# Where three V products stand behind stage A and D items, and an unfolded stage D for batch 2

## The chip, the cores and the metric

One Trainium2 chip, one core. The time is what the device takes for one execution of the whole program, in microseconds (us); less is better. Each kernel has several runs, and their median stands for it. One further execution was taken by the hardware profiler; all views of the trace are of that one.

## The reference

The input x is (8, 3072, 256) in float32. The first half takes the real part of a two-dimensional Fourier transform of each batch (over the 3072 positions and the 256 features); the second half is a channel mix on its result:

```
X   = fft(fft(x, axis=1), axis=2).real
xk  = mu_k * X + (1 - mu_k) * X_prev      # X_prev: X moved on by one position, zeros first
xr  = mu_r * X + (1 - mu_r) * X_prev
k   = relu(xk @ w_k)                      # 256 -> 1024
v   = (k * k) @ w_v                       # 1024 -> 256
out = sigmoid(xr @ w_r) * v
```

## The kernel before, in words

**The channel mix** is the bulk of the work and sets the beat. A batch has 3072 positions, in six chunks of 512 (`chunks`, line 997: 48 in all, three of the first half of the positions and three of the mirrored half per batch). A chunk takes four steps, so there are 192 steps and a few more to empty the pipeline. In every step TensorE makes one *K piece* (`k_piece`, lines 830 to 837): four products of 512 columns, two of the chunk's eight blocks of k, into one psW buffer. ScalarE (ACT) empties that with a relu into `rl`. Every second step VectorE (DVE) squares two steps' worth of `rl` into `k2` (`square`, line 845). Five steps behind, every step has a *V tile* (`v_tile`, lines 859 to 867): eight products of 256 columns for 128 positions, which read `k2` of an earlier chunk. Its first four products read the first half of `k2`, its last four the second half; so the first V tile of a chunk (steps 21, 25, 29, ...) waits for the latest square. Two V tiles share a psV buffer, and `v_out` (line 888) multiplies them with the sigmoid `r` on VectorE and issues the output DMAs. Every fourth step has an `r_item` (eight products, one sigmoid on ACT). PSUM is held as three psW buffers of 1024 columns, taken in turn by K pieces, r items and all transform items, and two psV buffers of 512.

**The transform** of later batches is cut into items and put between these steps. `fold` (line 160) adds a row of x to its mirrored partner (`p`). From `p`, `quarters_1` and `quarters_2` (lines 177 to 202, six VectorE operations per half h) fold the features twice more; `butterfly` (line 205, two operations per half) folds them once. Both write `eo`. Stage A (`a_half`, line 610, with `a_slots_0`) multiplies `eo` with half-array products (48 of 128 rows) and evicts to `a`, once per (h, e). Stage D turns `a` into `g_all`. It has two forms: `d_half` (line 672), for input folded twice, with products of 64 rows, two row halves of the array side by side, and two ACT evictions per item; it needs the table `w_d`, which `quarter_tables` (line 549) builds with one product, four ACT copies and two VectorE memsets on row 64. The other is `d_item` (line 665), for input folded once, with products of all 128 rows and one eviction per item. Batch 1 uses `d_item` and `butterfly`, batches 2 to 7 `d_half` and the quarters. `turned` (line 692) is one small product on `g_all` and an ACT copy. Stage C (`c_pairs`, line 738) makes `pq`; `halves` (line 751) adds and subtracts its two parts on VectorE to y, `diff` (line 762) takes differences of y, and `mix` (lines 770 to 813) makes from y and these the x that K pieces and r items read.

**The order** is written out by hand. `at(step, ...)` puts an item into a step, in class "x" if it uses TensorE (behind the K piece, ahead of the V tile) and else in class "w" (VectorE work and loads, at the step's end). `event(step, ...)` puts a stretch of stage A, C or D items behind the V tile of its step. The loop at lines 1140 to 1164 issues, per step: K piece, x items, V tile, event items, w items, output, square. After an event of three items the V tile of the *next* step follows at once: `event` then adds that step to `early_v` (line 995), and the loop skips it at its own place. An event that begins with `a_slots_0` is left out of that rule. `EVENTS` (line 1001) gives the steps of a batch's events, from 24 b for the transform of batch b + 2: 29 (three D items), 33 (the fourth, two C items), 41 (two C items and the first A item of the next batch), 45 (the other three A items). `pin_order` keeps each engine to the order of issue.

Of the kernel before, what the change touches and what calls it, by code (L numbers as in the profile page):

```python
# [39 lines left out]
def kernel(  # L40
# [916 lines left out]
    for a in range(2):  # L957
        t = x_t["t", a] = mix_pool.tile([P, 24, 64], FP16, name=f"t{a}")
# [25 lines left out]
    def at(step, f, *args):  # L984
        work.setdefault((step, "x" if f in (a_item, a_sum, d_item, d_small, c_item, c_tiles, turned, minus_0, r_item, quarter_tables) else "w"),
                        []).append((f, args))
# [3 lines left out]
    early_v = set(range(17, 20))  # L990

    def event(step, *items):
        work.setdefault((step, "e"), []).extend((f[0], f[1:]) for f in items)
        if len(items) > 2 and items[0][0] is not a_slots_0:
            early_v.add(step + 1)
# [5 lines left out]
    EVENTS = (29, 33, 41, 45)  # L1001
# [64 lines left out]
    at(17, c_tiles, 1)  # L1066
    at(17, fold, 2, 0)
    event(18, (c_item, 1, 0, 8), (c_item, 1, 8, 8))
    at(18, quarters_1, 2, 0)
    at(19, quarters_2, 2, 0)  # L1070
    at(18, fold, 2, 1)
    event(20, (c_item, 1, 16, 8), (c_item, 1, 24, 4), (a_half, 2, 0, 0))
    at(19, diff, 1, 0, 12)
    at(20, r_item, (0, 1, 1))
    at(23, a_half, 2, 0, 1)
    at(20, mix, 1, 0, 0, 0, 0, 12)
    at(21, quarters_1, 2, 1)
    at(22, quarters_2, 2, 1)
    at(21, mix, 1, 0, 0, 1, 0, 12)
    at(22, diff, 1, 12, 26)  # L1080
    at(21, load_gate)
# [6 lines left out]
    at(26, mix, 1, 0, 1, 0)  # L1088
    event(27, (a_slots_0, 2), (a_half, 2, 1, 0), (a_half, 2, 1, 1))
    at(28, r_item, (1, 0, 0))  # L1090
    at(28, mix, 1, 0, 1, 1)
    at(22, quarter_tables)
    at(30, mix, 1, 1, 1, 0)
    at(31, mix, 1, 1, 1, 1)
    at(32, r_item, (1, 0, 1))
    for n, c in enumerate(chunks[8:]):
        at(4 * n + 36, r_item, c)
    for b in range(B):
        s0 = 24 * b

        for n, st0 in enumerate((2, 4, 6, 8) if b > 1 else ()):
            at(s0 + st0, mix, b, n // 2, 1, n % 2)
        if b and b + 3 < B:
            at(s0 + 22, load_gate)
            for h in range(2):
                at(s0 + 22, load_xh, b + 3, h)
        t = b + 2
        if t < B:
            if b:
                at(s0 + 9, fold, t, 0)  # L1110
                at(s0 + 10, quarters_1, t, 0)
                at(s0 + 11, quarters_2, t, 0)
                at(s0 + 12, fold, t, 1)
                at(s0 + 14, quarters_1, t, 1)
                at(s0 + 15, quarters_2, t, 1)
            c = [(c_pairs, t, 8 * n, (8, 8, 8, 4)[n], "A") for n in range(4)]
            d = [(d_half, t, n) for n in range(4)]
            a = [(a_half, t + 1, h, e) for h in range(2) for e in range(2)] if t + 1 < B else []
            at(s0 + 32, turned, 0, 12)
            at(s0 + 37, turned, 12, 13)  # L1120
            event(s0 + EVENTS[0], *d[:3])
            event(s0 + EVENTS[1], d[3], *c[:2])
            event(s0 + EVENTS[2], *c[2:], *a[:1])
            if a:
                event(s0 + EVENTS[3], (a_slots_0, t + 1), a[2], a[3], a[1])
        t = b + 1
        if b and t < B:
            at(s0 + 16, halves, t, 0, 15)
            at(s0 + 18, halves, t, 15, 27)
            for a in range(2):  # L1130
                at(s0 + 19 + a, diff, t, 0, 26, (a,))
                at(s0 + 21 + a, mix, t, 0, 0, a)
            at(s0 + 24, mix, t, 1, 0, 0)
            at(s0 + 25, mix, t, 1, 0, 1)
# [62 lines left out]
```

## Time and profile before

| | |
|---|---|
| median of 3 runs | 434.36 us (433.93 to 434.51) |
| profiled execution | 434.02 us, span 432.2 us |
| granted TensorE clock, mean | 0.999 |
| PE busy | 421.7 us, 4018 matmuls |
| VectorE busy | 371.3 us, 594 instructions |
| ScalarE busy | 329.8 us, 414 instructions |
| DMA | 42.08 MB, mean 97 GB/s |

The span runs from the first to the last instruction; the 1.8 us beside it lie around the program. A view of the trace names an instruction by engine, line of the kernel, operation, and output and input tiles. PE is TensorE's products, ACT is ScalarE, DVE is VectorE. In a timeline the columns are start and length in us, then the engine, line and operation, the shapes, how many instructions were put together, and in brackets how long the engine sat idle before the first and what ended that. Products on PE are pipelined, so what one costs is read from start to start, not from its length. In the list of waits the numbers are us in total, times, and the longest. In a row of stretches the numbers are the stretch, its length, and the busy time of each engine with its instructions in brackets (PE, weight loads, VectorE, ScalarE, GpSimd), the clock, and the DMA share and rate; with a line of the kernel chosen, only that line's engine is given. In a row of a group, the numbers behind the bar are busy us and mean ns of one.

### The profile page before, as it was taken

What the parts mean: (1) busy time and instruction counts of PE and PEld (TensorE: products, weight loads), DVE (VectorE), ACT (ScalarE), POOL (GpSimd) and SP (SyncE); (2) the same over time, 40 slices, a digit from 0 to 9 for tenths busy, and PEclk for the clock granted to TensorE, in tenths of its full rate; (3) what the DMA queues carried; (4) which work ended last, traced back from release to release, by engine and by line L of the source; (5) the groups of instructions that cost most, each with busy time, mean ns of one, the idle gap of its engine ahead of it and who ended that gap; (6) DMA issues with size and microseconds to landing.
All of it is one profiled execution on the core that took longest, in us unless ns stands there. A gap on an engine that the chain in (4) does not pass through costs nothing.

```text
span 432.2 us, 9708 instructions
## 1 busy us (share of the span) xinstructions
PE 421.7 (98%) x4018; PEld 294.5 (68%) x4018; DVE 371.3 (86%) x594; ACT 329.8 (76%) x414; POOL 62.3 (14%) x97
## 2 busy tenths in 40 slices
PE   8999999999999999999999999999999999999996
PEld 3767766667666776766677677667766766766775
DVE  8999999999987999979989899888998756997543
ACT  7889897886878878687786967778686887666661
POOL 7488402000050002300041000500000000000000
PEclk9999999999999999999999999999999999999999
DMA  8789956323385224932368223762332323223333
GB/s 174 103 121 197 219 124 129 75 53 70 74 155 137 52 63 80 193 78 57 76 116 175 66 55 69 146 146 52 73 74 49 74 52 73 61 65 73 70 75 97
DMA packets 35104, 42.08 MB, mean 97 GB/s; under 512 B 4114, under 2 KB 31092, under 8 KB 35060
## 3 DMA queue, kind: packets, MB, share of 16 engines
q1 hardware_dynamic: 27488, 25.41, 24.2%
q0 software_dynamic: 7264, 15.80, 21.8%
q8 instruction: 31, 0.51, 0.5%
q10 hardware_dynamic: 308, 0.26, 0.2%
q14 instruction: 13, 0.11, 0.1%
HBM read 32.08 MB, written 25.17 MB: 132 GB/s over the span
## 4 chain that ended last, share of the span: by engine, by line
PE 88%; DVE 5%; ACT 4%; issue 1%; POOL 0%; POOLq 0%; DVEq 0%
PE psW L825 36%; PE psV L866 33%; PE psW L852 9%; PE psV L878 3%; ACT g_all L574 2%; PE psW L746 1%; DVE k L845 1%; ACT a L574 1%; PE psW L235 1%; PE psW L679 1%; DVE x L790 1%; DVE o L888 1%; PE psW L635 1%; DVE t L779 1%; PE psW L617 1%
## 5 line engine op out<-in xcount | busy, mean ns | idle before, releaser
L835 ACT ACTIVATE rl<-psW 128x1024 f16<-128x1024 f32 x192 | 194.3, 1030 | 85.7 <-PE psW L825 80.8
L825 PE MATMUL psW<-x,wk 128*128 128x512 f16 (+1 forms) x776 | 194.9, 377 | 3.4 <-ACT a L574 2.8
L866 PE MATMUL psV<-wv_sb,k 128*128 128x256 f16 x1424 | 184.7, 273 | 1.5 <-DVE k L845 1.5
L866 PEld LDWEIGHTS <-k 128*128 128x128 f16 x1424 | 136.6, 98 | 41.9 <-DVE k L845 2.3
L845 DVE TENSOR_TENSOR k<-rl 128x2048 f16<-128x2048 f16 (+1 forms) x100 | 115.6, 1157 | 37.1 <-ACT rl L835 36.8
L825 PEld LDWEIGHTS <-wk 128*128 128x128 f16 x776 | 75.3, 98 | 58.4 <-issue 5.1
L888 DVE SCALAR_TENSOR_TENSOR o<-psV,r 128x512 f32<-128x512 f32 (+1 forms) x97 | 65.8, 681 | 11.7 <-PE psV L866 10.6
L790 DVE TENSOR_TENSOR x<-y,t 128x1536 f16<-128x1536 f16 (+3 forms) x74 | 62.1, 846 | 2.1
L852 PE MATMUL psW<-wr,x 128*128 128x256 f16 x384 | 49.8, 273 | 0.0
L857 ACT ACTIVATE r<-psW 128x1024 f16<-128x1024 f32 x48 | 48.9, 1019 | 0.8 <-PE psW L852 0.8
L852 PEld LDWEIGHTS <-x 128*128 128x128 f16 x384 | 37.5, 98 | 14.3
L494 POOL IOTA gate<- 1x1 int32 x7 | 2.3, 323 | 205.4 <-DVE gate L493 205.4
L574 ACT ACTIVATE g_all<-psW 128x512 f16<-128x512 f32 (+5 forms) x67 | 28.8, 513 | 2.0 <-PE psW L679 1.6
L574 ACT ACTIVATE a<-psW 128x832 f16<-128x832 f32 x31 | 25.5, 865 | 1.4 <-PE psW L617 1.2
L172 DVE TENSOR_TENSOR p<-xp,xm 112x2304 f16<-112x2304 f16 (+6 forms) x19 | 21.7, 1141 | 0.5 <-DMA xm<-in_x_dram,idx 0.5
L779 DVE TENSOR_SCALAR t<-d,muf_t 128x1536 f16<-128x1536 f16 (+3 forms) x42 | 21.6, 527 | 0.1
L574 ACT ACTIVATE pq<-psW 128x1024 f16<-128x1024 f32 (+1 forms) x24 | 20.8, 922 | 1.2 <-PE psW L746 1.2
L141 POOL DMA_INDIRECT xm<-in_x_dram,idx_g x18 | 20.0, 1110 | 5.5 <-issue 5.2
L779 DVE TENSOR_SCALAR t<-d,mu_m 128x1536 f16<-128x1536 f16 x32 | 19.8, 619 | 0.0
L183 DVE TENSOR_TENSOR t<-p 112x576 f16<-112x576 f16 (+3 forms) x36 | 17.2, 533 | 0.0
L767 DVE TENSOR_TENSOR d<-y 128x1664 f16<-128x1664 f16 (+5 forms) x19 | 16.7, 881 | 0.2 <-ACT y L574 0.2
L759 DVE TENSOR_TENSOR y<-pq 128x960 f16<-128x960 f16 (+1 forms) x24 | 13.5, 605 | 2.7 <-ACT pq L574 2.4
(149 smaller groups left out, 226.1 us busy)
## 6 DMA issues: line engine op xcount, KB each, us to landing
out_dram<-o SPq DMA_DIRECT2D x189, 128.0 KB, 2.4
xp<-in_x_dram POOLq DMA_DIRECT2D x12, 216.0 KB, 4.5
xp<-in_x_dram POOLq DMA_DIRECT2D x13, 192.0 KB, 7.7
xp<-in_x_dram POOLq DMA_DIRECT2D x2, 384.0 KB, 7.0
wv_sb<-in_moe_w_v_dram POOLq DMA_DIRECT2D x1, 512.0 KB, 8.8
xp<-in_x_dram SPq DMA_DIRECT2D x1, 480.0 KB, 4.1
xp<-in_x_dram POOLq DMA_DIRECT2D x1, 432.0 KB, 5.2
xm<-in_x_dram,idx_g POOLq DMA_INDIRECT x18, 7.9
```

Source lines behind the costliest of these rows:

```text
L141: nc.gpsimd.indirect_dma_start(dst, None, src, bass.IndirectOffsetOnAxis(ap=idx, axis=0))
L172: V.tensor_tensor(out=p[:, q0:q0 + n], in0=xp[:, q0:q0 + n], in1=_v(xm, o + 256, [(-256, n), (-1, 256)]), op=ALU.add)
L574: nc.scalar.activation(out=out_ap, in_=in_ap, func=AF.Copy)
L779: V.tensor_scalar(out=dst, in0=src, scalar1=mu, scalar2=None, op0=ALU.mult)
L790: V.tensor_tensor(out=_v(x_t[b, j, m], o, [(64 * step, hi - lo), (step, 64)]), in0=y_t[b][:, lo + 3 * m:hi + 3 * m, a], in1=x_t["t", a][:, ...
L825: nc.tensor.matmul(out=st["k", ds][:, 512 * hs + lo:512 * hs + hi], lhsT=wk_sb[m][a][:, 128 * fc:128 * fc + 128], rhs=xk[:, a, 512 * i + l ...
L835: nc.scalar.activation(out=st["rl"][:, 2 * ds:2 * ds + 2], in_=st["k", ds].rearrange("p (f t) -> p f t", f=2), func=AF.Relu, bias=0.0, sca ...
L845: V.tensor_tensor(out=k2_t[c][:, lo:hi], in0=r, in1=r, op=ALU.mult)
L852: nc.tensor.matmul(out=ps[:, 256 * tb:256 * tb + 256], lhsT=x_t[b, 1, m][:, a, 512 * i + 128 * tb: 512 * i + 128 * tb + 128], rhs=wr_sb[m] ...
L857: nc.scalar.activation(out=st["r", c], in_=ps, func=AF.Sigmoid)
L866: nc.tensor.matmul(out=st["v", tb - h][:, 256 * h:256 * h + 256], lhsT=k2_t[c][:, fc, 128 * tb:128 * tb + 128], rhs=wv_sb[:, fc], start=(f ...
L888: V.scalar_tensor_tensor(out=o.rearrange("p a b -> p (a b)")[:, 0:256 * n], in0=st["v", t0][:, 0:256 * n], scalar=16.0, in1=st["r", c][:, ...
```

## The change

In the stretches of b = 1 and later, the V tile of step 24 b + 31 moves to the end of step 30 (behind the K piece of step 30, ahead of that of step 31), and the V tile of step 24 b + 46 to the end of step 45, right behind the three stage A items there. Batch 2 gets `butterfly` in place of the quarters, and its stage D as four `d_item`s, one each in steps 28, 29, 31 and 33 ahead of the V tile, and one `turned` over all 13 columns in step 34. Its C items then stand in events of steps 37 and 41, each with one stage A item of batch 3; the event of step 45 keeps two stage A items. V tiles no longer stand early in steps 30 and 34 of b = 0, but in 38 and still in 42. `quarter_tables`, which batch 3 is then the first to need, moves from step 22 to step 42.

```diff
-    at(18, quarters_1, 2, 0)
-    at(19, quarters_2, 2, 0)
+    at(18, butterfly, 2, 0)
...
-    at(21, quarters_1, 2, 1)
-    at(22, quarters_2, 2, 1)
+    at(21, butterfly, 2, 1)
...
     at(28, r_item, (1, 0, 0))
+    at(28, d_item, 2, 0)
     at(28, mix, 1, 0, 1, 1)
-    at(22, quarter_tables)
+    at(29, d_item, 2, 1)
     at(30, mix, 1, 1, 1, 0)
+    at(31, d_item, 2, 2)
     at(31, mix, 1, 1, 1, 1)
     at(32, r_item, (1, 0, 1))
+    at(33, d_item, 2, 3)
+    at(34, turned, 0, 13)
+    at(42, quarter_tables)
...
             d = [(d_half, t, n) for n in range(4)]
             a = [(a_half, t + 1, h, e) for h in range(2) for e in range(2)] if t + 1 < B else []
+            if not b:
+                event(s0 + 37, *c[:2], a[0])
+                event(s0 + 41, *c[2:], a[1])
+                event(s0 + 45, (a_slots_0, t + 1), *a[2:])
+                continue
             at(s0 + 32, turned, 0, 12)
             at(s0 + 37, turned, 12, 13)
             event(s0 + EVENTS[0], *d[:3])
+            early_v.add(s0 + EVENTS[0] + 2)
             event(s0 + EVENTS[1], d[3], *c[:2])
             event(s0 + EVENTS[2], *c[2:], *a[:1])
             if a:
                 event(s0 + EVENTS[3], (a_slots_0, t + 1), a[2], a[3], a[1])
+                early_v.add(s0 + EVENTS[3] + 1)
```

## Prediction

> **What bounds the kernel now.** I read the page's totals first, then its chain of waits. K46 stands for the K piece of step 46, V46 for the V tile of that step; in the stretch of a batch index b, step 29 means step 24b + 29.
>
> ```profile
> span 432.2 us, 9708 instructions
> ...
> PE 421.7 (98%) x4018; PEld 294.5 (68%) x4018; DVE 371.3 (86%) x594; ACT 329.8 (76%) x414; POOL 62.3 (14%) x97
> ...
> PE 88%; DVE 5%; ACT 4%; issue 1%; POOL 0%; POOLq 0%; DVEq 0%
> ```
>
> TensorE is busy for 98% of the span and carries 88% of the chain that ends last. So two things alone can move the end: the products on PE, and the holes between them. The list of waits on PE tells of the holes.
>
> ```profile
> PE psW L825 <- ACT a L574: 2.8, 5, 0.6
> PE psV L866 <- DVE k L845: 1.5, 3, 0.9
> ```
>
> Five times a K product (L825) waits until ScalarE has emptied a stage A buffer; three times a V product (L866) waits for VectorE's square. The timeline shows where. First the end of the step-45 items of b=1 (stage A of batch 4), PE, then ACT:
>
> ```profile
> 168.28 0.78 PE L617 MATMUL psW<-w_hh,eo 48*128 48x52 f16 x46
> 169.61 1.02 PE L825 MATMUL psW<-x,wk 128*128 128x512 f16 x4 [0.55 <-ACT a L574]
> ...
> 168.69 2.38 ACT L574 ACTIVATE a<-psW 128x832 f16<-128x832 f32 x3 [0.21 <-PE psW L617]
> ```
>
> The stretch of half-array products ends at about 169.06. K of step 46 needs one of the three psW buffers, and the first of three evictions on ACT has to free it: a hole of 0.55. Next the step-29 items of batch 4 (stage D), V of step 29 to V of step 31:
>
> ```profile
> 184.37 1.04 PE L866 MATMUL psV<-wv_sb,k 128*128 128x256 f16 x8
> 185.34 0.87 PE L679 MATMUL psW<-w_d,a 64*128 64x64 f16 x48
> 186.15 1.05 PE L866 MATMUL psV<-wv_sb,k 128*128 128x256 f16 x8
> 187.03 2.11 PE L825 MATMUL psW<-x,wk 128*128 128x512 f16 x8
> 188.98 1.04 PE L866 MATMUL psV<-wv_sb,k 128*128 128x256 f16 x8
> ...
> 185.79 3.36 ACT L574 ACTIVATE g_all<-psW 128x512 f16<-128x512 f32 x6 [0.20 <-PE psW L679]
> ```
>
> V takes 0.88 from start to start; ahead of the 64-row products it took 0.97, so entering them costs 0.10 and leaving them almost nothing. The two K pieces after V30 should take 2 x 0.865 = 1.73 but take 1.95: the second waits 0.22 for the buffer of the second D item (six evictions in 3.36, the fourth done about 2.28 after 185.79, at 188.07). The list of waits misses this, because modelled matmul ends cover it. Last, V of steps 21, 25 and 29, where batch 2 is prepared:
>
> ```profile
> 63.39 0.61 PE L866 MATMUL psV<-wv_sb,k 128*128 128x256 f16 x4 [0.23 <-DVE k L845]
> ...
> 72.12 0.60 PE L866 MATMUL psV<-wv_sb,k 128*128 128x256 f16 x4
> 73.65 0.61 PE L866 MATMUL psV<-wv_sb,k 128*128 128x256 f16 x4 [0.93 <-DVE k L845]
> ...
> 82.61 0.61 PE L866 MATMUL psV<-wv_sb,k 128*128 128x256 f16 x4 [0.31 <-DVE k L845]
> ```
>
> Four products start within 0.44, so the second half of V25, due at 72.56, came 1.09 late: the idle shown plus 0.16. The others, so corrected, are 0.39 and 0.47: 1.95 in all.
>
> **The change, part by part.** (1) *Step 45, b = 1 to 4.* V46 now fills the hole. It needs nothing new: its psV buffer is V45's, its k2 was squared before V45. V takes 0.89 behind such a stretch (186.15 to 187.03), so K46 starts at 169.94, K47 at 170.80, K48 at 171.67. The three evictions take 2.38 from 168.69, so they are done at about 169.5, 170.3 and 171.1: all three K pieces find their buffer free, by 0.4 or more. K46 came at 169.61 with V46 behind it; that pair now ends at 170.80 instead of 171.34. Gain 0.54 each, 2.15.
>
> (2) *Step 29, b = 1 to 5.* V31 goes between K30 and K31, so K31 starts at 188.77, after 188.07. K32 then needs the third D item's buffer at 189.63; that is free at 189.15. Gain 0.22 each, 1.08. V31 opens a psV buffer that the output of step 28 has emptied. Relu and square of step 31 lose nothing, since ACT is busy with stage D until 189.15 in any case.
>
> (3) *VectorE, batch 2.* quarters_1 and quarters_2 go, two additions per half come. Removed (L183, L198, L200, L202 in that stretch), then an added operation at each size (the larger by its twin at L183):
>
> ```profile
> 55.00:71.00 16.00, 2.87 (x6) 1.00 0.51 110
> ...
> 55.00:71.00 16.00, 1.44 (x2) 1.00 0.51 110
> ...
> 55.00:71.00 16.00, 0.48 (x2) 1.00 0.51 110
> ...
> L211 DVE TENSOR_TENSOR eo<-p 96x1024 f16<-96x1024 f16 x1 | 0.7, 683 | 0.0
> L183 DVE TENSOR_TENSOR t<-p 112x1152 f16<-112x1152 f16 x1 | 0.8, 752 | 0.0
> ```
>
> L198 and L200 give the same row, so 2.87 + 2 x 1.44 + 0.48 = 6.23 goes, 2 x 0.752 + 2 x 0.683 = 2.87 comes; net 3.36, some 3.0 from start to start. Half of that, about 1.4, lies ahead of the square that V21 reads, all of it ahead of those for V25 and V29. VectorE has next to no idle in this stage, so it comes earlier by just that:
>
> ```profile
> 52.00:88.00 36.00, 34.48 (x385) 23.56 (x382) 34.85 (x57) 30.14 (x41) 2.39 (x4) 1.00 0.51 110
> ...
> 59.07 1.94 ACT L835 ACTIVATE rl<-psW 128x1024 f16<-128x1024 f32 x2
> ```
>
> Its busy time is the third sum, 34.85 of 36. TensorE itself comes 0.39 earlier from V21 on and 1.48 from V25 on, less than the 3.0. All three holes close: 1.95. What is late next is the relu that a square reads. For V21 it ends at 61.0 (59.07 + 1.94), the square 1.14 later at 62.15, and V21's second half is due at 63.00; for V25 the relu (67.60 in part 6) ends at 68.6, and its square is due near 72.1. Neither takes the wait over. The gate of batch 3's load, a memset in VectorE's queue at step 21, comes as much earlier; its data are read at step 36, so nothing follows from that.
>
> (4) *Stage D of batch 2.* It goes from 52 half-array products to 26 full ones.
>
> ```profile
> 49.47 0.89 PE psW L657 x16
> ...
> 194.32 0.23 PE L679 MATMUL psW<-w_d,a 64*128 64x64 f16 x4
> 194.39 0.65 PE L746 MATMUL psW<-m_cs,g_all 64*128 64x64 f16 x32
> ```
>
> Removed: 0.81 + 0.07 for the products, 0.10 and 0.02 at the edges: 1.00. Added: 26 x 0.0556 = 1.45, without edges, one item to a step, evicted between relus. The first stands behind the sigmoid products of step 28, which cover the stage A evictions that it reads; ACT has 30.14 of 36 in the stage above, so there is room for its four evictions. `turned` at step 34 follows a K piece (0.86), which covers the last, smallest one. Net +0.45. Its K31 hole (0.22) goes. One `turned` product less: -0.03.
>
> (5) *Stage A of batch 3.* One item moves from step 45 to 41, one from 41 to 37; step 45 of b=0 keeps two, so K46 finds a free buffer, as after step 27, which has two and is not among the five waits. Gain 0.55; the moved products +0.05.
>
> (6) *The tables' step moves from 22 to 42,* and here the change pays. It issues one product, four ACT copies and two VectorE memsets, and no DMA; SP's and POOL's queues keep their order. All of it now stands right behind the step-41 items. Rows of before: PE; ACT; the copies at their old place with the relu behind them; DVE.
>
> ```profile
> 109.21 1.05 PE L866 MATMUL psV<-wv_sb,k 128*128 128x256 f16 x8
> 110.10 1.89 PE L825 MATMUL psW<-x,wk 128*128 128x512 f16 x8
> 111.82 1.04 PE L866 MATMUL psV<-wv_sb,k 128*128 128x256 f16 x8
> ...
> 121.99 1.03 PE L825 MATMUL psW<-x,wk 128*128 128x512 f16 x4
> ...
> 109.00 1.51 ACT L574 ACTIVATE pq<-psW 128x1024 f16<-128x1024 f32 x2 [0.19 <-PE psW L746]
> 110.40 0.87 ACT L574 ACTIVATE a<-psW 128x832 f16<-128x832 f32 x1
> 111.16 1.95 ACT L835 ACTIVATE rl<-psW 128x1024 f16<-128x1024 f32 x2
> ...
> 66.73 0.25 ACT L574 ACTIVATE w_d<-w_eo 64x64 f16<-64x64 f16 x1
> ...
> 67.60 1.02 ACT L835 ACTIVATE rl<-psW 128x1024 f16<-128x1024 f32 x1
> ...
> 110.55 1.03 DVE L759 TENSOR_TENSOR y<-pq 128x768 f16<-128x768 f16 x2 [0.25 <-ACT pq L574]
> 115.51 0.69 DVE L888 SCALAR_TENSOR_TENSOR o<-psV,r 128x512 f32<-128x512 f32 x1 [0.21 <-PE psV L866]
> ...
> 119.43 0.96 DVE L790 TENSOR_TENSOR x<-y,t 128x1536 f16<-128x1536 f16 x1
> ```
>
> On before's clock: K42 ends at 110.96 and the table product (0.06, the same as at its old place, so no term of the sum) takes the psW buffer that K43 would have had. K43 needs the next one, which the stage A eviction frees at 111.27 (110.40 + 0.87); due at 111.02, it waits 0.29 with the semaphore. The copies take 67.60 - 66.73 = 0.87 behind the relu of step 42, so end at 112.98. The memsets overwrite a row of what the copies write and wait for them; behind them queue `halves`, the output of step 42, both `diff`s, the squares of 43 and 45, and both `mix`es that make x for K48. The memsets take 0.14, so `halves` starts at 113.12 instead of 110.55. The idle 0.21 takes some back, the rest of the queue is shut; the last mix ends at 120.39 + 2.36 = 122.75. K48's second product, which reads it, is due at 121.99 + 0.22 + 0.35 + 0.04 - 0.55 - 0.25 = 121.80 (0.35 is K43's delay with the table product, 0.04 V45's, 0.55 part 5's hole, 0.25 the 16 stage A products that leave step 45). So K48 waits 1.0; V45, whose square ends level with its need, about 0.04. Together +1.33. This wait is nowhere in the trace, so its ends: 0, if VectorE has slack that I don't see, and 2.6 + 0.3, if all of the hold reaches TensorE. I take 1.33, since each piece of it is a distance between rows.
>
> [...]
>
> *Sum:* -2.15 - 1.08 - 1.95 + 0.45 - 0.22 - 0.03 - 0.55 + 0.05 + 1.33 = -4.15. The profiled execution took 434.02 (span 432.2 and 1.8 around it): 429.87. It lies 0.34 under the median of the three runs, 434.36, which would give 430.21. I predict **430.0**.
>
> **The rivals.** (A) *The holes only move:* with V gone from behind K46 or K31, two K pieces stand back to back, and the second waits, as K31 does now. Against it: the buffers are free 0.4 ahead. If it did, (1) and (2) would go: 429.87 + 2.15 + 1.08 = 433.1. (B) *The hold is harmless:* VectorE's queue has slack before K48, or the copies come earlier: 429.9 - 1.3 = 428.6. For it: 14% of VectorE's span is idle; against it: none but 0.21 of it lies between halves and mix. (C) *Squares stay late:* V21 to V29 wait on the relus, not on VectorE's queue: 429.9 + 1.95 = 431.8. Against it: in that stretch VectorE is never idle. (D) *Slower:* the hold at step 42 grows. Without it the sum is -5.48; each us that ACT reaches the copies later comes through to K48 whole, once the 1.3 of slack is used. To be slower by 0.87, the loss must be 6.35, the copies 5.0 us later than I place them; at 6 us later, 435.9. Against it: before those evictions ACT had idled 0.19. (E) *Nothing:* gains and a hold of 5.5 cancel: 434.
>
> **How the numbers follow.** Forecast 0.60 (429.2 to 431.0), A 0.07, B 0.14, C 0.09, D 0.05, E 0.05. The range takes in forecast, B and C and with them both ends of part 6 (428.5 and 431.4): 428.4 to 432.2, for 0.83. About 0.2% (0.87 us) is what a measurement can tell from no change. Faster 0.90, same 0.05, slower 0.05.
>
> **What the profile of after would show.** Right: the five waits of L825 on ACT's stage A gone, no wait of L866 on squares between 60 and 83 us, K30, V31, K31 without a hole in each batch, a new wait near 118 us of L825 on VectorE's x (L790's line) of about 1 us, VectorE idle about 2.5 before its memsets, and K43 0.3 late. Wrong: K47 or K32 waiting on ACT (A), no wait at K48 (B), V waits left before 83 us (C), a K48 wait of several us or a square wait at V45 to V53 (D). A granted clock under 0.99 would void the sum.

## The result, and the profile after

The changed kernel takes 429.71 us (median of 4 runs, 429.43 to 430.0) against 434.14 for the kernel before (4 runs, 433.83 to 434.51): 4.43 us less, ratio 0.9898 (95% interval 0.9881 to 0.9915). The profiled execution took 429.43 with a span of 427.7. The forecast was 430.0, with a range of 428.4 to 432.2.

The page of the changed kernel, its totals and its chain:

```profile
span 427.7 us, 9640 instructions
...
PE 420.9 (98%) x3991; PEld 295.4 (69%) x3991; DVE 367.8 (86%) x586; ACT 328.6 (77%) x409; POOL 61.7 (14%) x97
...
PE 94%; DVE 3%; issue 1%; POOL 0%; ACT 0%; POOLq 0%; DVEq 0%
```

PE's busy time fell by only 0.8 us, the span by 4.5: what went is waiting. The chain says the same: TensorE now carries 94% of it, and ScalarE's 4% is gone. The list of waits on PE of the changed kernel, the rows that matter in the loop:

```profile
PE psW L825 <- DVE x L790: 0.7, 1, 0.7
```

The eight waits that stood there before (five on stage A evictions, three on squares) are gone, and a single new one has come: a K piece on VectorE's x. (K43's wait of 0.30, read below from start to start, is not in the list.) Now the places. Step 45 of b=1, PE and ACT:

```profile
166.89 0.22 PE L603 MATMUL psW<-w_hh,eo 112*128 112x52 f16 x2
167.04 0.78 PE L617 MATMUL psW<-w_hh,eo 48*128 48x52 f16 x46
167.74 1.05 PE L866 MATMUL psV<-wv_sb,k 128*128 128x256 f16 x8
168.63 1.89 PE L825 MATMUL psW<-x,wk 128*128 128x512 f16 x8
...
167.45 2.38 ACT L574 ACTIVATE a<-psW 128x832 f16<-128x832 f32 x3 [0.21 <-PE psW L617]
```

V46 stands behind the stage A products, and the K pieces of steps 46 and 47 follow each other without a gap (a line of eight, no idle in front). The evictions still take 2.38, but TensorE has other work meanwhile. V46 starts 0.70 after the 46 products began. Step 29 of b=2:

```profile
184.30 1.05 PE L866 MATMUL psV<-wv_sb,k 128*128 128x256 f16 x8
185.18 1.03 PE L825 MATMUL psW<-x,wk 128*128 128x512 f16 x4
186.04 1.04 PE L866 MATMUL psV<-wv_sb,k 128*128 128x256 f16 x8
186.92 1.89 PE L825 MATMUL psW<-x,wk 128*128 128x512 f16 x8
```

From start to start V30, K30, V31 and the K pair take 0.88, 0.86, 0.88 and 1.73: no hole. Batch 2's preparation, V21, V25 and V29 and one stage D item, and the row of busy times from 52 to 88 us:

```profile
62.75 1.05 PE L866 MATMUL psV<-wv_sb,k 128*128 128x256 f16 x8
...
71.86 1.04 PE L866 MATMUL psV<-wv_sb,k 128*128 128x256 f16 x8
72.73 1.03 PE L825 MATMUL psW<-x,wk 128*128 128x512 f16 x4
...
80.79 0.61 PE L657 MATMUL psW<-w_eo,a 128*128 128x128 f16 x8
81.24 1.04 PE L866 MATMUL psV<-wv_sb,k 128*128 128x256 f16 x8
82.11 1.03 PE L825 MATMUL psW<-x,wk 128*128 128x512 f16 x4
...
52.00:88.00 36.00, 36.00 (x376) 25.80 (x373) 34.41 (x50) 30.78 (x35) 2.71 (x4) 1.00 0.55 117
```

The V tiles are whole again (eight products in one row; V25 takes 0.87 instead of 1.98). A full stage D item costs 0.45. PE is busy for all of the 36 us. Last the tables' step at 42, DVE, ACT and PE:

```profile
107.44 1.22 DVE L845 TENSOR_TENSOR k<-rl 128x2048 f16<-128x2048 f16 x1
111.57 0.12 DVE L556 MEMSET w_d<- 1x32 f16 x2 [2.91 <-ACT w_d L574]
111.70 1.03 DVE L759 TENSOR_TENSOR y<-pq 128x768 f16<-128x768 f16 x2
...
120.17 0.96 DVE L790 TENSOR_TENSOR x<-y,t 128x1536 f16<-128x1536 f16 x1
...
111.28 0.22 ACT L574 ACTIVATE w_d<-psW 64x64 f16<-64x64 f32 x1
...
109.53 0.22 PE L551 MATMUL psW<-w_eo,same 128*128 128x128 f16 x1
109.90 1.02 PE L825 MATMUL psW<-x,wk 128*128 128x512 f16 x4
...
120.12 0.38 PE L825 MATMUL psW<-x,wk 128*128 128x512 f16 x1
121.18 0.81 PE L825 MATMUL psW<-x,wk 128*128 128x512 f16 x3 [0.68 <-DVE x L790]
```

VectorE stands idle for 2.91 until ACT's last copy, then works through its queue; the last mix ends at 121.13, and the second product of K48, due at 120.34, starts at 121.18: 0.84 late. The table product itself (0.06) is followed 0.36 later by K43: 0.30 of waiting.

### The profile page after: what moved, and what is told of

Read it like the earlier page. It is cut to its first block, busy times and chain, and to the rows that moved or that the text cites. A ratio compares the mean times of both kernels' runs of the same rounds, so it can differ in the third digit from the quotient of the medians.

```text
span 427.7 us, 9640 instructions
## 1 busy us (share of the span) xinstructions
PE 420.9 (98%) x3991; PEld 295.4 (69%) x3991; DVE 367.8 (86%) x586; ACT 328.6 (77%) x409; POOL 61.7 (14%) x97
## 4 chain that ended last, share of the span: by engine, by line
PE 94%; DVE 3%; issue 1%; POOL 0%; ACT 0%; POOLq 0%; DVEq 0%
PE psW L825 38%; PE psV L866 36%; PE psW L852 10%; PE psV L878 3%; PE psW L746 1%; PE psW L679 1%; PE psW L617 1%; PE psW L235 1%; PE psW L657 1%; PE psW L635 1%; DVE k L845 1%; PE psW L714 1%; PE psV L378 1%; DVE y L759 1%; DVE d L767 0%
## 5 line engine op out<-in xcount | busy, mean ns | idle before, releaser
L866 PE MATMUL psV<-wv_sb,k 128*128 128x256 f16 x1424 | 184.2, 273 | 0.0
L574 ACT ACTIVATE g_all<-psW 128x512 f16<-128x512 f32 (+8 forms) x62 | 28.9, 542 | 1.3 <-PE psW L679 1.0
L878 PE MATMUL psV<-wv_sb,k 128*128 128x256 f16 x112 | 14.7, 273 | 0.0
```

The lines of the kernel that those rows point to most:

```text
L574: nc.scalar.activation(out=out_ap, in_=in_ap, func=AF.Copy)
L866: nc.tensor.matmul(out=st["v", tb - h][:, 256 * h:256 * h + 256], lhsT=k2_t[c][:, fc, 128 * tb:128 * tb + 128], rhs=wv_sb[:, fc], start=(f ...
L878: nc.tensor.matmul(out=st["v", tb - h][:, 256 * h:256 * h + 256], lhsT=k2_t[c][:, fc, 128 * tb:128 * tb + 128], rhs=wv_sb[:, fc], start=fc ...
```

## The experiments

The theory was the one on record: parts that add up, each in its own place. The rivals were that the holes only move, that the square waits went through something other than VectorE's relief, and that K48's wait has another cause than the memsets. In the first four kernels below, the kernel before, run beside them, took 434.33; in the next four 434.50; in the last three 434.21.

**V46 alone** (the kernel before, and):

```diff
+                if b:
+                    early_v.add(s0 + EVENTS[3] + 1)
```

> The kernel before with one edit: V46 stands right behind the three stage A items of step 45, for b = 1 to 4. Theory: four holes of 0.6 us each close and no other opens, so 432.0 (before 434.14 less 2.1 to 2.5), and the list of waits shows one wait of a K piece on a stage A eviction (b = 0) in place of five. Rival (the holes only move): K47, now straight behind K46, waits for the next eviction; at most 0.2 us less than before, and still five waits.

Measured: 431.98, ratio 0.9946 (0.9932 to 0.9960), 2.35 less. The list of waits:

```profile
PE psV L866 <- DVE k L845: 1.5, 3, 0.9
...
PE psW L825 <- ACT a L574: 0.6, 1, 0.6
```

Four of the five ACT waits are gone and none has come at K47; the squares' three are untouched. The holes do not move.

**V31 alone** (the kernel before, and):

```diff
+            if b:
+                early_v.add(s0 + EVENTS[0] + 2)
```

> The kernel before with one edit: V31 stands between K30 and K31, for b = 1 to 5. Theory: five holes of 0.22 close, 433.05 (-1.1), K32 follows K31 without a gap. Rival (the holes only move): K32 waits in place of K31, 434.1.

Measured: 433.32, ratio 0.9975 (0.9965 to 0.9986), 1.01 less. So this part too is worth what its hole was, although the list of waits had never shown it.

**Batch 2 alone** (the changed kernel without both `early_v.add` lines).

> The changed kernel without its two early V tiles for b = 1 and later, so batch 2's part alone: butterfly, full stage D, the regrouped events, the tables at step 42. Theory: -1.95 of square waits, -0.62 of step 45's hole, -0.2 of K31's, +0.45 of stage D, +1.14 of the tables' step; 433.2, about 0.9 under before. With e1 and e2 the three parts should add up to the whole: 4.4. Rival: the parts overlap, and batch 2 alone gives over 2 us.

Measured: 433.29, ratio 0.9974 (0.9965 to 0.9983), 1.04 less. The three parts give 2.35 + 1.01 + 1.04 = 4.40 against 4.43 for the whole. The traces say the same: from the first K piece to the last product the three kernels take 2.38, 1.11 and 1.24 less than the kernel before, 4.73 together, and the whole change 4.70. The parts don't overlap.

**Tables at step 35:**

```diff
-    at(42, quarter_tables)
+    at(35, quarter_tables)
```

> The changed kernel with quarter_tables at step 35 in place of 42. At 35 no stretch of items stands ahead of it, ScalarE is ahead of VectorE, and K36 finds another psW buffer free. Theory (the hold): K43's wait of 0.30 and K48's of 0.84 go, VectorE's memsets wait for nothing; 428.6, 1.1 under the changed kernel. Rival: the wait of K48 has another cause (VectorE simply has too much to do between steps 42 and 46), and it stays; 429.4 at best.

Measured: 428.47, ratio 0.9868 (0.9853 to 0.9883). K43's wait and K48's are both gone from the trace. But the memsets do wait, against the theory: they still hold VectorE for 0.98 (it was less far behind than I had thought), and V37, which takes 0.87 undisturbed, takes 1.16, with 0.10 of that the entry into the C products behind it:

```profile
94.90 0.13 DVE L556 MEMSET w_d<- 1x32 f16 x2 [0.98 <-ACT w_d L574]
...
97.27 1.23 PE L866 MATMUL psV<-wv_sb,k 128*128 128x256 f16 x8
98.43 0.64 PE L746 MATMUL psW<-m_cs,g_all 64*128 64x64 f16 x32
```

**The memsets on GpSimd,** the rest of the step still at 42:

```diff
-            V.memset(_v(w_d[64:65], 64 + k, [(2, 32)]), 2.0 * k - 1.0)
+            nc.gpsimd.memset(_v(w_d[64:65], 64 + k, [(2, 32)]), 2.0 * k - 1.0)
```

> The changed kernel with the tables' two memsets on GpSimd in place of VectorE; the rest of the step stays at 42. Theory: VectorE goes past the copies, so K48's wait of 0.84 goes, while K43's 0.30 (a matter of the psW buffers) stays; 428.85, about 0.85 under the changed kernel. Rival: K48 waits because the four copies make the relus and squares late, not because of the memsets; then it stays, 429.7.

Measured: 428.68, ratio 0.9869 (0.9853 to 0.9884). DVE, POOL and PE of this kernel, and last the stage A eviction of step 41 in the changed kernel (ACT):

```profile
108.96 1.03 DVE L759 TENSOR_TENSOR y<-pq 128x768 f16<-128x768 f16 x2 [0.46 <-ACT pq L574]
...
111.46 0.19 POOL L556 MEMSET w_d<- 1x32 f16 x2 [42.79 <-ACT w_d L574]
...
109.37 0.22 PE L551 MATMUL psW<-w_eo,same 128*128 128x128 f16 x1
109.74 1.02 PE L825 MATMUL psW<-x,wk 128*128 128x512 f16 x4
...
108.98 0.87 ACT L574 ACTIVATE a<-psW 128x832 f16<-128x832 f32 x1
```

The copies still end at about 111.5, but `halves` now starts at 108.96, and K48 waits for nothing. K43 keeps its delay: 0.37 behind the table product. So the memsets in VectorE's queue made K48's wait. K43's fits the psW buffer: in the changed kernel the stage A eviction ends at 109.85 (108.98 + 0.87) and K43 starts at 109.90, and here they stand at 109.68 and 109.74. That is timing only; the profile does not name what ended this wait.

**The copies twice** (a loop of two around the four copies; the work is repeated, the values are the same).

> The changed kernel with the tables' four copies made twice, so the memsets on VectorE are released 0.87 later. Theory: the slack between the hold and K48 is used up, so each further microsecond reaches K48 whole; its wait goes from 0.84 to 1.7, the time to 430.55. Rival: VectorE makes up for it on the way, under 0.3 more, 430.0 at most.

Measured: 430.86, ratio 0.9919 (0.9904 to 0.9933). By the ratios that is 0.2% over the changed kernel, 0.9, though the two intervals overlap; the trace is plainer (DVE and PE; this kernel's lines behind the loop are one higher):

```profile
112.81 0.13 DVE L557 MEMSET w_d<- 1x32 f16 x2 [3.98 <-ACT w_d L575]
...
115.41 0.60 PE L867 MATMUL psV<-wv_sb,k 128*128 128x256 f16 x4
116.71 0.61 PE L867 MATMUL psV<-wv_sb,k 128*128 128x256 f16 x4 [0.70 <-DVE k L846]
...
PE psW L826 <- DVE x L791: 0.8, 1, 0.8
```

The hold grew from 2.91 to 3.98, by 1.07 and not by the 0.87 that I had reckoned. All of it reaches TensorE: from the start of K43 to the r products of step 48 it takes 13.01, where the changed kernel takes 11.92, 1.09 more. But it comes at other places. V45, which reads the square between the hold and K48, is now 0.86 late; the r products of step 44, which start right behind the last copy, are 0.13 late; and since TensorE has lost that already, K48's wait is 0.92, hardly more than its 0.84. The rival (under 0.3 more) is refuted; that K48's own wait would double does not hold either.

**VectorE's work put back** (changed kernel):

```diff
+    at(18, quarters_1, 2, 0)
...
+    at(21, quarters_1, 2, 1)
```

> The changed kernel with three of the removed VectorE operations per half put back as extra work on a scratch tile (quarters_1 of batch 2 beside its butterfly, 2.7 us in all, read by nobody). Theory: the square waits of V21, V25 and V29 come back for the most part, some 1.6, and the time is 431.3. Rival: the waits went because stage D is spread over four steps, not because VectorE has less to do; 429.7.

Measured: 430.68, ratio 0.9911 (0.9897 to 0.9925). That is 0.6 over the changed kernel by the ratios and 1.0 by the medians, and the two intervals overlap, so the time alone does not refute the rival. The trace does; the wait on squares is back:

```profile
63.33 1.22 PE L866 MATMUL psV<-wv_sb,k 128*128 128x256 f16 x8
...
73.78 0.61 PE L866 MATMUL psV<-wv_sb,k 128*128 128x256 f16 x4 [0.57 <-DVE k L845]
...
82.73 1.04 PE L866 MATMUL psV<-wv_sb,k 128*128 128x256 f16 x8
```

The first row is V21, 0.18 late (1.06 to the next start at 64.39, instead of 0.88), the second is V25's second half, 0.73 late, and the last is V29, not late at all. So VectorE's work is what V21 and V25 had waited for, but I expected 1.6 and got 0.9. The extra work left some of the relief, 0.36 at V25 (1.09 less 0.73). And V29's 0.47 is covered: its square ends at 82.69, 0.48 ahead of its second half (due 0.44 after 82.73), while the two full D items that the change puts ahead of it take 0.45 each. Without them it would have waited, by this estimate, about 0.4.

**The folded stage D spread** (the kernel before with quarters and tables in their places, `d_half` counted among the items that stand ahead of the V tile, and):

```diff
+    at(28, d_half, 2, 0)
+    at(29, d_half, 2, 1)
+    at(31, d_half, 2, 2)
+    at(33, d_half, 2, 3)
+    at(34, turned, 0, 13)
...
+            if not b:
+                event(s0 + 37, *c[:2], a[0])
+                event(s0 + 41, *c[2:], a[1])
+                event(s0 + 45, (a_slots_0, t + 1), *a[2:])
+                continue
```

> The kernel before with batch 2's folded stage D (half-array products, quarters kept, tables at step 22) spread over steps 28, 29, 31 and 33 and its events regrouped as in the change. Theory: VectorE has as much to do as before, so the three square waits stay; step 45's hole (0.62) and K31's (0.22) go; four entries and exits of half-array products cost 0.36 more; 433.75, 0.5 under before. It tells the worth of the spreading and regrouping without the unfolding: the full products cost 0.1 more on TensorE and save 1.95 through VectorE. Rival: the spreading does the good by itself, and this has 432 or less.

Measured: 433.63, ratio 0.9980 (0.9971 to 0.9989). PE from V25 to V29:

```profile
74.15 0.61 PE L866 MATMUL psV<-wv_sb,k 128*128 128x256 f16 x4 [0.93 <-DVE k L845]
...
80.56 0.41 PE L679 MATMUL psW<-w_d,a 64*128 64x64 f16 x16
80.91 1.05 PE L866 MATMUL psV<-wv_sb,k 128*128 128x256 f16 x8
81.79 1.03 PE L825 MATMUL psW<-x,wk 128*128 128x512 f16 x4
82.75 0.41 PE L679 MATMUL psW<-w_d,a 64*128 64x64 f16 x16
83.09 1.05 PE L866 MATMUL psV<-wv_sb,k 128*128 128x256 f16 x8
```

The waits of V21 and V25 are there as before (0.38 and 1.09), with all of VectorE's work. But V29, the last row, is whole: the D products ahead of V28 and V29 (0.35 each to the next start, and 0.10 for each entry) push it back by more than the 0.47 that it had waited. Spreading alone closes that hole, at the price of the products that stand in it.

**D behind the V tiles** (changed kernel, all four so):

```diff
-    at(28, d_item, 2, 0)
+    event(28, (d_item, 2, 0))
```

> The changed kernel with batch 2's four full stage D items behind the V tiles of steps 28, 29, 31 and 33 in place of ahead of them. It asks what closed V29's hole of 0.47: in the kernel with the folded D spread (all of VectorE's work kept) the hole was gone too, since the D products ahead of V28 and V29 push V29 back by 0.7. Theory (VectorE's relief alone is enough): V29 still waits for nothing, 429.7. Rival (only the products ahead of it cover it): V29 waits 0.4 to 0.5 for the square, 430.2.

Measured: 429.80, ratio 0.9900 (0.9883 to 0.9916), beside 429.70 for the changed kernel. V29, now ahead of its D item, and the square that its second half reads (DVE):

```profile
80.75 1.04 PE L866 MATMUL psV<-wv_sb,k 128*128 128x256 f16 x8
81.63 0.61 PE L657 MATMUL psW<-w_eo,a 128*128 128x128 f16 x8
...
78.45 1.22 DVE L845 TENSOR_TENSOR k<-rl 128x2048 f16<-128x2048 f16 x1
```

It waits for nothing. The D item of step 28 (0.45) still stands ahead of it, behind V28, so the edit does not quite take the two covers apart; the rows do. The square ends at 79.67, and V29's second half is due at 81.19, 1.52 later; without that D item too it would be 1.07. Two things thus covered V29 in the change, and VectorE's relief is enough by itself.

**Tables at 35 and the memsets on GpSimd** (both edits above).

> The changed kernel with quarter_tables at step 35 and its memsets on GpSimd. At 35 the memsets still held VectorE for 0.98 and V37 waited 0.18 for a square. Theory: that goes too, 428.3, 1.35 under the changed kernel and the least of all. Rival: no difference from the tables at 35 alone, 428.5.

Measured: 428.64, ratio 0.9872 (0.9855 to 0.9888), not told apart from the tables at 35 alone (0.9868) or the memsets on GpSimd alone (0.9869). So in the time the rival's forecast holds: it is not the least of all. V37 no longer waits (0.97 to the next start instead of 1.16), but from the first K piece to the last product the profiled execution takes 404.38, as with the tables at 35 alone (404.35): it lost 0.21 near 40 us, at V products between the stage A products of batch 1, which the edit does not touch.

**The changed kernel again.**

> The changed kernel itself, beside the two above on the same chip: 429.7, K43 waiting 0.3 and K48 0.84.

Measured: 429.70, ratio 0.9899 (0.9882 to 0.9915), with the same two waits. The three variants of the tables' step all lie under it, by 1.0 to 1.2 by the medians and 1.2 to 1.3 by the ratios, and none of their runs is as slow as its fastest: about that much of the change's gain had been given back.

## Why the prediction was right

Main loop alone, from the first K piece to the last product, the profiled executions took 410.06 and 405.36: 4.70 less, where the sum said 4.15. (The changed kernel's first K piece came 0.17 later, a matter of start-up, so that the spans differ by 4.5.) By its steps:

1. *Step 45:* predicted 0.54 a time, measured 0.61 to 0.62, so 2.45 for four instead of 2.15. The mechanism was right; the hole was mis-sized. I took the end that the profile gives for the last stage A product (169.06) for the point at which the next can start. With V46 behind them the 46 products need 0.70 to the next start, not the 0.78 of their row: the hole is longer by the overlap than the idle time that the profile gives. V46 alone gave 2.35, and 2.38 in its trace.
2. *Step 29:* predicted 1.08, measured 5 x 0.22 in the trace and 1.01 by itself.
3. *VectorE:* predicted 1.95. V21 fell from 1.28 to 0.88, V25 from 1.97 to 0.87, V29's half-wait of 0.47 went: 1.97. The cause is shown for V21 and V25 by the work put back. For V29 the prediction named VectorE alone, and its relief would have been enough; but the D products ahead of it covered it as well, which the prediction did not see.
4. *Stage D:* predicted 1.45 for the full products, measured 3 x 0.45 + 0.11 = 1.46; `turned` and K31's hole went as said.
5. *Step 45 of b=0:* its hole is 0.62 too, where 0.55 was forecast; the 16 products that leave the step were worth 0.19, not 0.25.
6. *The tables:* predicted 1.33, measured 0.30 + 0.84 = 1.14. K43 was 0.29 by the forecast. K48 was to wait 1.0; VectorE idled 2.91 ahead of the memsets, where about 2.5 was forecast, but `halves` to the end of the last mix took 9.43 instead of 9.84. So VectorE made up 0.2 more of the hold than the one idle time of 0.21 that I counted: before the change, the operations behind the two `diff`s had each started some 0.1 later than they could, without the timeline listing it (the square at 113.14 follows the relu that ended at 113.11). V45 lost nothing. The term also rests on VectorE starting nothing from behind the waiting memsets; the rows show just that: `halves`, whose input ScalarE had finished by 109.09, started at 111.70, and at 108.96 with the memsets on GpSimd. In the kernel before, too, VectorE idled 0.25 ahead of `halves` (110.55), though the V product that the operation behind it reads had ended at 110.26.

The sum of the measured terms is -2.45 - 1.08 - 1.97 + 0.46 - 0.22 - 0.03 - 0.62 + 0.01 + 1.14 = -4.76 against -4.70 in the trace (the 0.01: 0.20 more stage A and C products in step 37 than there were in 33, 0.19 less in 45). Of the rivals, A (the holes only move) and C (squares stay late) are refuted by the kernels with one part alone and with VectorE's work put back. B (the hold is harmless) is refuted by the memsets on GpSimd. D's premise, that each further microsecond comes through whole, held for a further 1.07, though nearly all of it showed ahead of K48. E would have needed a loss of 5.5 at the tables' step; it was 1.14.

What stays open: whether the last 0.2 us between the variants of the tables' step are real, since their intervals overlap; and what held K43 is read from timing alone.

## What to carry to other kernels

When the bound engine stands idle for a buffer that another engine is emptying, look for work that is ready and needs no such buffer, and put it there; its worth is the hole, taken from start to start and not from the idle column (here 0.62 against 0.55). Before moving a small step, look at every queue that it enters: two memsets, 0.12 us together, behind a copy on another engine held a queue for 2.9 us, and 0.84 of that reached the bound engine some 10 us later. Put such a thing on an engine with nothing behind it, or at a step where what it waits for is done sooner (here GpSimd, ratio 0.9869, and step 35, with a hold of 0.98 and 0.9868, against 0.9898).

## What the runs showed of the hardware

- The timeline's idle times on PE were too small here: the idle 0.55 was a hole of 0.62, and one of 0.22 wasn't listed, because the rows of products reach past the point at which the next could start (the row of the 46 stage A products is 0.78 long, V46 starts 0.70 after it began).
- Going from products of 128 rows to products of 64 or 48 cost 0.10 (V 0.97 to the next start in place of 0.87, r products 0.96 in place of 0.87), and coming back 0.01 to 0.02 (V 0.88 or 0.89), wherever it was read; products of 128 rows and 128 columns between K and V had no such cost (0.45 for eight, 0.056 each, V behind them 0.87).
- The first K piece started between 18.13 and 18.63 us in the profiled executions (18.15 in the kernel before, 18.32 in the changed one), all with the same start-up code. That spread of 0.5 us is more than twice the hole of a step 29 (0.22), so effects of this size are compared from the first K piece on, not by the span.
